# ScalarE's side work ahead of the products with v, maxima turned into rows where a phase opens, row tails copied by VectorE

## The chip, the cores and the metric

The kernel runs on one core of a Trainium2 chip. Its time is the device time of one execution in microseconds (us); lower is better. The engines of the core run side by side and meet at semaphores: TensorE (PE; PEld is its loading of weights), VectorE (DVE), ScalarE (ACT), GpSimd (POOL) and SyncE (SP), which here only issues DMAs.

## The reference

Attention over pooled queries feeds two gated or plain MLPs. The change touches the first part:

```python
q_pool = q.reshape(B, H, S // 2, 2, D).mean(axis=3)      # B=4, H=8, S=1152, D=64
scores = np.matmul(q_pool, k.transpose(0, 1, 3, 2)) / np.sqrt(D)
scores = scores - np.max(scores, axis=-1, keepdims=True)
attn = np.exp(scores)
attn = attn / (np.sum(attn, axis=-1, keepdims=True) + 1e-09)
out = np.matmul(attn, v)
# then: h = relu(x @ w_in); u, v = halves of h; v normed, mixed over time by w_spatial, u * that @ w_out
# then: u = x + (U V applied over time); out = u + relu(u @ w_ch1) @ w_ch2
```

The weights of the MLPs come in as 64-bit floats and are turned into pairs of 32-bit numbers on the chip.

## The kernel before

**Attention in pairs of heads.** 32 heads make 16 pairs (`j`, a *phase* of the program each). A pair has 576 pooled queries, in three thirds of 192 columns, so there are 48 units `u`; keys come in 9 chunks `c` of 128. The chunks of all units stand in one row, and four of them make a *group* `i` (108 groups). A group is two score tiles `s`: for each, 4 matmuls with k (L258) and 2 that take off the row of maxima `toprow` (L274, or L277 where two pairs meet), then an exponential on ScalarE (`expo`, L281) into `pt`. GpSimd adds up the `pt` tiles (`acc`, L288, L299, L302).

**Turns.** After every odd group come the products with v (`pv`, L309, 32 matmuls) of the two groups before it, and, where a unit ends, its sums (`sums`: L323 on TensorE, then the copy L327 on ScalarE). This text calls the stretch from one block of products to the next a *turn*: products, sums, a group, a group. VectorE inverts the sums in two halves (L331) and multiplies (`out`, L337) one turn later, which frees the bank `po`.

**Maxima.** The row of maxima is computed ahead, from rounded copies of q and k, in *pieces*: two matmuls of 512 columns (L171) and one maximum on VectorE (L193); a piece of the rest (L171 with 128 columns, in odd halves L201 too; L204, L213, L216, L217 on VectorE); and one over the query tail `qd` (L188, L189). `end` says how many pieces have to be done by a group, `some` places one. When a pair's maxima are there, `to_rows` turns them into a row: matmuls `tr` (L232, L239), a copy of 512 columns (L242) and two of the 64 tail columns (L249). Pieces, `tr` and score tiles share one ring of three PSUM slots, `ring`.

**Side work on ScalarE.** For the pair after next, `round_k` (L151) and `round_q` (L140, L145) copy k and the pooled q into the rounded form; `pool_q` (L134, GpSimd) makes that q. `also(i)` hands a tick to the preparation of the weights (`Weights.tick`): `phase` 0 is two ScalarE activations (L589, L590), 1, 2 and 4 are VectorE (L594, L598, L602), 3 is GpSimd (L600), 5 is a ScalarE copy (L674), 6 GpSimd (L679).

The order on every engine is the order in which this code is written (the schedule is manual), so an engine that waits holds up all that is written behind it. The MLP stages behind attention, from about 470 us on, are not touched.

Of the kernel before, what the change touches and what calls it, by code (L numbers as in the profile page):

```python
# [10 lines left out]
F32 = mybir.dt.float32  # L11
F32R = mybir.dt.float32r
ACTF = mybir.ActivationFunctionType
# [3 lines left out]
U32 = mybir.dt.uint32  # L17
# [20 lines left out]
def attention(tc, idf, q, k, v, xs, rounded, also):  # L38
# [13 lines left out]
    nc = tc.nc  # L52
    NP, D, _, _, T = q.shape
    S = k.shape[3]
    HP = NP // len(xs)
    KC = S // 128
# [13 lines left out]
    with ExitStack() as ctx, ExitStack() as sco:  # L70
# [14 lines left out]
        for e in range(2):  # L85
            p = slice(64 * e, 64 * e + 64)
# [23 lines left out]
        st = [dict() for _ in range(NP)]  # L110
# [19 lines left out]
        def pool_q(j, eng, c0=0, c1=T):  # L130
            s = st[j]
            if "q" not in s:
                s["q"] = ld.tile([128, T], F32, tag="q", name="q", bufs=3)
            eng.tensor_tensor(out=s["q"][:, c0:c1], in0=s["qraw"][:, 0, c0:c1], in1=s["qraw"][:, 1, c0:c1], op=ALU.add)  # L134

        def round_q(j, c0=0, c1=T):
            s = st[j]
            if "qr" not in s:
                s["qr"] = qrs[j % 2]
            nc.scalar.copy(s["qr"][:, c0:min(c1, 512)], s["q"][:, c0:min(c1, 512)])  # L140
            if c1 == T:
                s["qd"] = qds[j % 2]
                for e in range(2):
                    p = slice(D * e, D * e + D)
                    nc.scalar.copy(s["qd"][p, D * e:D * e + D], s["q"][p, 512:T])  # L145

        def round_k(j, c0=0, c1=S):
            s = st[j]
            if "kr" not in s:
                s["kr"] = krs[j % 2]  # L150
            nc.scalar.copy(s["kr"][:, c0:c1], s["k"][:, c0:c1])  # L151
# [6 lines left out]
        pieces = []  # L158
# [6 lines left out]
        upto = [sum(x[0] < u for x in pieces) for u in range(2 * NP + 1)]  # L165
# [55 lines left out]
        def to_rows(*us):  # L221

            j = us[0] // 2
            if us[0] % 2 == 0:
                st[j]["top"] = ld.tile([128, T], F32R, tag="toprow", name="toprow")
            t = st[j]["top"]
            rs = ring("tr")
            cs = [2 * (u % 2) + c for u in us for c in range(2)]
            for c in cs:
                for i in range(2):  # L230
                    p = slice(64 * i, 64 * i + 64)
                    nc.tensor.matmul(  # L232
                        rs[:, i, 64 * c:64 * c + 64], tops[j % 2][p, c].rearrange("p e d -> p (e d)"), idr[p],
                        start=True, stop=True,
                    )
            if us[-1] % 2:
                for i in range(2):
                    p = slice(64 * i, 64 * i + 64)
                    nc.tensor.matmul(  # L239
                        rs[:, i, 256:320], tops[j % 2][p, 4].rearrange("p e d -> p (e d)"), idr[p], start=True, stop=True  # L240
                    )
            nc.scalar.copy(  # L242
                t[:, 128 * cs[0]:128 * cs[-1] + 128].rearrange("p (c i x) -> p i c x", i=2, x=64),
                rs[:, :, 64 * cs[0]:64 * cs[-1] + 64].rearrange("p i (c x) -> p i c x", x=64),
            )
            if us[-1] % 2:
                for i in range(2):
                    p = slice(64 * i, 64 * i + 64)
                    nc.scalar.copy(t[p, 512:T], rs[p, i, 256:320])  # L249

        def scores(pair):

# [120 lines left out]
        groups = [chunks[i:i + G] for i in range(0, len(chunks), G)]  # L373

        at = [3 * KC * j // G for j in range(NP)]
        before = []

        smalls = {}
# [9 lines left out]
        j = 0  # L388
        for i, group in enumerate(groups):
            if j + 1 < NP and at[j + 1] == i:  # L390
                j += 1
            r = i - at[j]
            if r == 0:
                if j + 2 < NP:
                    load_k(j + 2)
                    load_q(j + 2)
                if j + 1 < NP:
                    load_v(j + 1)

            end = min(upto[2] + -(-upto[2] * (4 * (i | 1) + 8) // (3 * KC)), upto[2 * NP])  # L400
            if i < len(FIRST):
                end = min(end, FIRST[i])

            def some(beside=False, lag=0):
                if done[0] < end - lag:
                    piece(beside=beside)

            new = []
            if i == 2:
                new = [1]  # L410
            elif r == 0 and j:
                new = [2 * j, 2 * j + 1]
            for u in new:
                while done[0] < upto[u + 1]:
                    piece()
            if new:
                to_rows(*new)
            elif i % 2 == 0:
                some(True)
            for x in smalls.pop((i, 0), ()):  # L420
                x()
            ts = []
            for x in range(0, G, W):
                pair = group[x:x + W]
                ts.append((pair, scores(pair)))
                if i == 0 and x + W == G:
                    some()
                if i or x + W == G:
                    for y in ts:
                        less(*y)  # L430
                        expo(*y)
                    ts = []
            if i < len(FIRST):
                some(bool(i % 2))
            elif i % 2 == 0:
                some(lag=1)
            else:
                some(done[0] + 1 >= end)
                some(True)

            for _ in range(2 if i < 4 else 0):
                if done[0] < end:
                    piece(ps_s.tile([128, 2, 512], F32, tag="s", name="r1"))
            for x in smalls.pop((i, 1), ()):
                x()
            if i + 1 == len(groups):
                break
            if i == 0:
                round_q(1)
                round_k(1)  # L450
            if i % 2:
                for x in before:
                    pv(*x)
                before = []
                for u in sums_at.pop(i, ()):
                    sums(u)
            before = before + group
            also(i)
            if r == 2 and j + 2 < NP:
                pool_q(j + 2, nc.gpsimd)  # L460

            if r == 3 and j + 2 < NP:
                round_k(j + 2)
            if r == 4 and j + 2 < NP:
                round_q(j + 2)
        sco.close()
        for x in before:
            pv(*x)
# [30 lines left out]
class Weights:  # L499
# [5 lines left out]
    def __init__(self, nc, stages, most=1 << 30, keep=None):  # L505

        self.nc, self.stages, self.most, self.keep = nc, stages, most, keep
        self.units, self.free = [], []
        self.time = self.begun = self.loaded = self.staged = 0

        self.apart = 2

        self.late = 0

    def load(self, units=(), raws=()):

# [53 lines left out]
    def work(self, u, phase):  # L574

        nc = self.nc
        if phase == 5:  # L580
            u["hi"](u["st"])
        elif phase == 6:
            u["lo"](u["st"])
        elif not u["f32"]:
            lo, hi = u["raw"][:, :, 0], u["raw"][:, :, 1]
            if phase == 0:
                u["st"] = self.stages[self.staged % len(self.stages)][0:u["p"], 0:u["n"]]
                self.staged += 1
                nc.scalar.activation(u["st"], hi.bitcast(F32), ACTF.Abs, scale=2.0**-48)  # L589
                nc.scalar.activation(lo, lo.bitcast(U32), ACTF.Copy, scale=2.0**-29)  # L590
            st = u["st"]
            o = st.bitcast(I32)
            if phase == 1:
                nc.vector.tensor_scalar(  # L594
                    out=st, in0=st, scalar1=LEAST, scalar2=MOST, op0=ALU.max, op1=ALU.min, accum_out=LOWEST[0][0:st.shape[0]]
                )
            elif phase == 2:
                nc.vector.tensor_scalar(out=o, in0=o, scalar1=3, scalar2=None, op0=ALU.logical_shift_left)  # L598
            elif phase == 3:
                nc.gpsimd.tensor_tensor(out=o, in0=o, in1=lo, op=ALU.add)  # L600
            elif phase == 4:
                nc.vector.scalar_tensor_tensor(  # L602
                    out=o, in0=hi, scalar=-0x80000000, in1=o, op0=ALU.bitwise_and, op1=ALU.bitwise_or
                )
# [79 lines left out]
def gated_mlp(tc, idf, w_in, w_sp, b_sp, w_out, wU, wV, xs, us, last, soon, then, spill):  # L684
# [104 lines left out]
    w = Weights(nc, stages, keep=LAST)  # L789
    w.apart = 4  # L790
    w.late = 1

    yield yh.rearrange("p a t d -> p (a t d)")
    nc.gpsimd.memset(f(wst[64:128, 1, NT - 1]), 0.0)
    i = 0
    while not isinstance(i, str):
        if i == WEIGHTS:
            w.load(units, raws)
        if i >= WEIGHTS + 2:
            w.tick()  # L800
        if i == X_AT:
            load_x(0)
        i = yield
    w.end()

    e2 = room(right, "e2", side="right")
# [595 lines left out]
```

## Time and profile before

| | |
|---|---|
| median of 3 runs | 1123.17 us (1122.11 to 1123.65) |
| the profiled execution | 1123.47 us, of which the span 1121.5 us |
| PE busy over the span | 1103.0 us (98%) |
| PEld, DVE, ACT, POOL busy | 956.2, 578.1, 446.8, 541.1 us |
| chain that ended last | PE 50% of the span, no other engine over 3% |

Matmuls overlap in TensorE's pipeline, so a busy row has stretched matmuls in it too; a wait of TensorE shows first in its loading of weights, which runs ahead of the matmuls. A timeline row is: start, length, engine, line, operation, tiles and shapes, count, and in brackets the engine's idle time ahead of it with what ended it.

### The profile page before, as it was taken

The page shows a single profiled execution, that of the slowest core. Times are in us where ns is not written, and L with a number is a line of the kernel's source. Part 1 is how long each engine was busy: PE and PEld are TensorE (multiplying, and loading weights), DVE is VectorE, ACT ScalarE, POOL GpSimd, SP SyncE. Part 2 cuts the span into 40 slices and gives each one's busy share as a digit, 9 for nine tenths or more (in the row PEclk, how much of TensorE's full clock was granted, in tenths as well). Part 3 has the DMA queues.
Part 4 walks back from the last instruction along what each step waited for, and adds up shares of the span by engine and source line. Part 5 has one row for each costly group of instructions (what it writes and reads, how often), then busy time and mean ns, then how long its engine had stood idle before and what let it go on. Part 6 is the DMA issues. An engine that isn't in the chain of part 4 may idle for free.

```text
span 1121.5 us, 20408 instructions
## 1 busy us (share of the span) xinstructions
PE 1103.0 (98%) x8406; PEld 956.2 (85%) x8406; DVE 578.1 (52%) x933; ACT 446.8 (40%) x824; POOL 541.1 (48%) x421
## 2 busy tenths in 40 slices
PE   8999999999999999999999999999999999999998
PEld 6878878888778888798988989899998999999897
DVE  6767877766777785353465653469412121121211
ACT  4455565555665554452343443356311111111110
POOL 4678899898799796534364545357300000000000
PEclk9999999999999999999999999999999999999999
DMA  6334333325334311022233406345102010010000
GB/s 169 90 89 114 103 100 103 82 70 135 98 98 135 82 36 37 12 69 91 84 114 111 139 29 193 99 137 164 48 1 85 1 57 1 1 57 1 29 1 29
DMA packets 44847, 86.65 MB, mean 77 GB/s; under 512 B 6353, under 2 KB 21329, under 8 KB 44754
## 3 DMA queue, kind: packets, MB, share of 16 engines
q1 hardware_dynamic: 44754, 85.35, 25.8%
q8 instruction: 66, 1.08, 0.4%
q14 instruction: 27, 0.22, 0.1%
HBM read 66.98 MB, written 17.83 MB: 76 GB/s over the span
## 4 chain that ended last, share of the span: by engine, by line
PE 50%; DVE 3%; ACT 1%; DMA 1%; POOL 1%; issue 1%; SPq 0%; ACTq 0%; POOLq 0%; DVEq 0%
PE ph L1245 18%; PE py L1259 18%; PE py L1025 4%; PE pu L973 3%; PE pg L991 3%; PE pv L838 2%; DMA cw<-st 1%; PE pU L1008 1%; PE pt L1237 1%; DVE st L664 1%; POOL st L662 1%; PE pV L1050 1%; DVE bs L933 1%; POOL gt L491 0%; DVE xt L491 0%
## 5 line engine op out<-in xcount | busy, mean ns | idle before, releaser
L1245 PE MATMUL ph<-ut,w 128*128 128x384 f32 x1152 | 216.9, 336 | 0.0
L1259 PE MATMUL py<-w,h 128*128 128x512 f32 x864 | 216.7, 395 | 0.0
L1245 PEld LDWEIGHTS ph<-ut,w 128*128 128x128 f32 x1152 | 203.9, 188 | 8.4
L1249 DVE SCALAR_TENSOR_TENSOR h<-ph,h 128x384 fp32r<-128x384 f32 x96 | 53.5, 557 | 284.6 <-ACT h L1248 284.6
L281 ACT ACTIVATE pt<-s 128x768 f32<-128x768 f32 x216 | 172.0, 811 | 60.4 <-PE s L274 56.7
L193 DVE TENSOR_REDUCE m<-r 128x2 f32<-128x1024 f32 x128 | 154.9, 1222 | 76.0 <-PE r L171 75.8
L299 POOL TENSOR_TENSOR acc<-pt,acc 128x768 f32<-128x768 f32 x94 | 173.7, 1848 | 37.4 <-ACT pt L281 31.9
L258 PE MATMUL s<-q,k 64*128 64x192 f32 x1728 | 184.8, 332 | 1.5 <-DVE m L193 0.7
L1259 PEld LDWEIGHTS py<-w,h 128*128 128x128 f32 x864 | 159.9, 188 | 29.8
L1248 ACT ACTIVATE h<-ph 128x384 fp32r<-128x384 f32 x96 | 47.2, 492 | 301.7 <-PE ph L1245 300.1
L258 PEld LDWEIGHTS s<-q,k 64*128 64x128 f32 x1728 | 142.8, 187 | 18.0 <-ACT pt L281 9.3
L309 PE MATMUL po<-pt,v 128*64 128x192 f32 x1728 | 154.2, 330 | 1.0 <-DVE x L337 0.9
L309 PEld LDWEIGHTS po<-pt,v 128*64 128x64 f32 x1728 | 118.8, 137 | 31.1 <-issue 13.7
L299 POOL TENSOR_TENSOR acc<-pt 128x768 f32<-128x768 f32 x48 | 88.1, 1836 | 33.0 <-ACT pt L281 32.8
L274 PE MATMUL s<-toprow,yh 64*128 64x384 f32 x416 | 99.1, 470 | 1.0 <-ACT toprow L242 1.0
L331 DVE RECIPROCAL sum<-sum 128x96 f32<-128x96 f32 x96 | 70.8, 742 | 32.8 <-ACT sum L327 32.8
L171 PE MATMUL r<-yh 64*128 64x512 f32 (+1 forms) x384 | 68.2, 384 | 5.1 <-ACT pt L281 5.0
L327 ACT ACTIVATE sum<-po 128x192 f32<-128x192 f32 x48 | 15.9, 331 | 140.8 <-PE po L323 102.5
L991 PE MATMUL pg<-wst,vn 128*128 128x288 f32 x448 | 60.6, 295 | 0.6 <-DVE ut L997 0.6
L991 PEld LDWEIGHTS pg<-wst,vn 128*128 128x128 f32 x448 | 59.7, 188 | 1.0 <-DVE ut L997 0.9
L171 PEld LDWEIGHTS r<-yh 64*128 64x128 f32 x384 | 35.2, 185 | 24.7 <-ACT pt L281 11.7
L973 PEld LDWEIGHTS pu<-xt,wi 128*128 128x128 f32 x384 | 53.3, 188 | 2.1
(153 smaller groups left out, 1345.1 us busy)
## 6 DMA issues: line engine op xcount, KB each, us to landing
raw<-in_moe_w_ch_dram SPq DMA_DIRECT2D x28, 512.0 KB, 3.8
v<-in_v_dram SPq DMA_DIRECT2D x16, 576.0 KB, 4.1
qraw<-in_q_dram SPq DMA_DIRECT2D x30, 288.0 KB, 5.6
k<-in_k_dram SPq DMA_DIRECT2D x30, 288.0 KB, 4.5
x<-x SPq DMA_DIRECT2D x48, 96.0 KB, 2.2
xn<-x SPq DMA_DIRECT2D x4, 1152.0 KB, 5.8
out_dram<-un SPq DMA_DIRECT2D x18, 256.0 KB, 2.1
raw<-in_moe_w_in_dram SPq DMA_DIRECT2D x8, 512.0 KB, 5.9
```

What stands on the lines that cost most here:

```text
L171: nc.tensor.matmul(o, s["qr"][p, q0:q0 + 128], s["kr"][p, k0:k0 + n], start=True, stop=True)
L193: nc.vector.tensor_reduce(out=m[:, c, :, k0 // PW], in_=r, axis=AX.X, op=ALU.max, negate=True)
L258: nc.tensor.matmul(t[:, e, N * x:N * x + N], s["k"][p, 128 * c:128 * c + 128], s["q"][p, q0:q0 + N], start=x == 0, stop=False,)
L274: nc.tensor.matmul(t[:, e, 0:2 * N], first[p], m, start=False, stop=True)
L281: nc.scalar.activation(x, t[:, :, 0:W * N], ACTF.Exp, scale=SC)
L299: nc.gpsimd.tensor_tensor(out=a, in0=x, in1=jb["t"] if c < 4 else a, op=ALU.add)
L309: nc.tensor.matmul(jb["o"][D * e:D * e + D, 0:N], st[u // 3]["v"][:, e, c], jb["p", c][:, e], start=c == 0, stop=c == KC - 1,)
L331: nc.vector.reciprocal(out=t, in_=t)
L973: nc.tensor.matmul(p[:, 0:HT], wi[0][:, a, k, 128 * m:128 * m + 128], xt[:, c, k, HT * h:HT * h + HT], start=i == 0, stop=i == 3 * KD - 1,)
L991: nc.tensor.matmul(p[:, 0:HT], vn[:, a, s, 128 * m:128 * m + 128], wst[:, c, s, sl], start=s == 0 and i == 0, stop=s == NT - 1 and i == 1,)
L1245: nc.tensor.matmul(p[:, 0:BT], w1s[m][:, a, k], ut[i][:, c, k], start=j == 0, stop=j == 3 * KD - 1)
L1259: nc.tensor.matmul(py[i][c], h[:, a, 128 * c:128 * c + 128], w2s[m][:, e], start=m == 0 and a + e == 0, stop=m == KM - 1 and a == 1,)
```

## The change

In `attention`, at the end of an odd group, the weights' tick, `round_k` and `round_q` (now both in the same odd group of a phase, r = 3 or 4) are written ahead of the products with v; before, they stood behind the products and the sums. In `Weights`, phases 0 and 5 of a tick don't issue their ScalarE instructions at once: `on_act` holds them, and `also(None)` issues what is held, which happens only in odd groups, ahead of the tick and again ahead of the products. `to_rows` is called only in an even group, right behind the products of the turn before (`turns`), with no piece between; a phase that opens with an odd group gets its row one group earlier. The pieces are due a group earlier (12 for 8 in `end`), and none is placed before its pair is rounded. The row's tail columns are copied by VectorE.

```diff
-                    nc.scalar.copy(t[p, 512:T], rs[p, i, 256:320])
+                    nc.vector.tensor_copy(out=t[p, 512:T], in_=rs[p, i, 256:320])
...
+        turns = {i - i % 2: j for j, i in enumerate(at) if j}
...
-            end = min(upto[2] + -(-upto[2] * (4 * (i | 1) + 8) // (3 * KC)), upto[2 * NP])
+            end = min(upto[2] + -(-upto[2] * (4 * (i | 1) + 12) // (3 * KC)), upto[2 * NP])
...
-                if done[0] < end - lag:
+                if done[0] < end - lag and "qr" in st[pieces[done[0]][0] // 2]:
                     piece(beside=beside)
...
-            elif r == 0 and j:
-                new = [2 * j, 2 * j + 1]
+            elif i in turns:
+                new = [2 * turns[i], 2 * turns[i] + 1]
...
             if i % 2:
+                also(None)
+            also(i)
+            if r == 2 and j + 2 < NP:
+                pool_q(j + 2, nc.gpsimd)
+            if r == 3 + at[j] % 2 and j + 2 < NP:
+                round_k(j + 2)
+                round_q(j + 2)
+            if i % 2:
+                also(None)
                 for x in before:
                     pv(*x)
                 before = []
                 for u in sums_at.pop(i, ()):
                     sums(u)
             before = before + group
-            also(i)
-            if r == 2 and j + 2 < NP:
-                pool_q(j + 2, nc.gpsimd)
-
-            if r == 3 and j + 2 < NP:
-                round_k(j + 2)
-            if r == 4 and j + 2 < NP:
-                round_q(j + 2)
...
+    def act(self):
+        for x in self.held:
+            x()
+        self.held = []
+
+    def on_act(self, x):
+        if self.held is None:
+            x()
+        else:
+            self.held.append(x)
...
         if phase == 5:
-            u["hi"](u["st"])
+            self.on_act(lambda: u["hi"](u["st"]))
...
+        if i is None:
+            w.act()
+        elif i >= WEIGHTS + 2:
             w.tick()
```

(Phase 0 goes through `on_act` in the same way; behind attention the held list is emptied and switched off.)

On ScalarE, around the opening of the pair with groups 13 to 19; before, two groups of exponentials (L281, two tiles each) with side work between them:

```order
L151 CAST yh<-k 128x1152
L281 ACTIVATE pt<-s 128x768 x2
L589 ACTIVATE st_114<-raw_110 128x512
L590 ACTIVATE raw_110<-raw_110 128x512
L140 CAST yh<-q 128x512
L145 CAST yh<-q 64x64 x2
L281 ACTIVATE pt<-s 128x768 x4
L242 CAST toprow<-tr 128x2x4x64
L249 CAST toprow<-tr 64x64 x2
```

The same place after; the exponentials of a turn stand together, side work stands behind them and ahead of the copy of the sums, L242 stands ahead of a turn's exponentials, and L249 is gone from this engine:

```order
L281 ACTIVATE pt<-s 128x768 x4
L151 CAST yh<-k 128x1152
L140 CAST yh<-q 128x512
L145 CAST yh<-q 64x64 x2
L327 ACTIVATE sum<-po 128x192
L281 ACTIVATE pt<-s 128x768 x4
L606 ACTIVATE st_114<-raw_110 128x512
L607 ACTIVATE raw_110<-raw_110 128x512
L242 CAST toprow<-tr 128x2x4x64
L281 ACTIVATE pt<-s 128x768 x4
```

On TensorE in the turn with groups 12 and 13, before, from the last products on (the `tr` of the phase stands between its two groups, behind a piece; numbers tell the buffers apart):

```order
L309 MATMUL po_843<-pt_791,v_277 64x192 x4
L171 MATMUL r_861<-yh_95 128x512 x2
L258 MATMUL s_866<-q_212,k_170 128x192 x4
L274 MATMUL s_866<-toprow_576,yh_95 128x384 x2
L258 MATMUL s_878<-q_212,k_170 128x192 x4
L274 MATMUL s_878<-toprow_576,yh_95 128x384 x2
L171 MATMUL r_888<-yh_95 128x512 x2
L232 MATMUL tr_902<-yh_95 128x64 x8
L239 MATMUL tr_902<-yh_95 128x64 x2
L258 MATMUL s_916<-q_212,k_170 128x192 x4
```

After, the `tr` stands right behind the products, and the piece between products and scores is gone from there:

```order
L309 MATMUL po_844<-pt_794,v_277 64x192 x4
L232 MATMUL tr_862<-yh_95 128x64 x8
L239 MATMUL tr_862<-yh_95 128x64 x2
L258 MATMUL s_876<-q_212,k_170 128x192 x4
L274 MATMUL s_876<-toprow_576,yh_95 128x384 x2
L258 MATMUL s_888<-q_212,k_170 128x192 x4
L274 MATMUL s_888<-toprow_576,yh_95 128x384 x2
L171 MATMUL r_898<-yh_95 128x512 x2
```

Of the 15 rows of maxima that are made after the first, 8 move like this; the other 7 stood there already. GpSimd and SP run the same instructions in the same order as before. TensorE runs the same matmuls.

On VectorE, after, at a later opening: the two tail copies stand behind the weights' work (L613, L621) and ahead of the first half of the next inversion.

```order
L337 TENSOR_TENSOR x<-po,sum 128x192
L193 TENSOR_REDUCE m<-r 128x2
L613 TENSOR_SCALAR pair,lowest<-pair 128x512
L621 SCALAR_TENSOR_TENSOR st_115<-raw_111,st_115 128x512
L249 CAST toprow<-tr 64x64 x2
L331 RECIPROCAL sum<-sum 128x96
```

Before, the same stretch has no L249; the rest of it is as it was.

## Rows read from the trace of the kernel before

**Rows 1.** Windows: start and end, length, busy and count by engine, clock, DMA.

```profile
40.00:470.00 430.00, 423.08 (x4651) 350.22 (x4650) 303.54 (x448) 242.90 (x408) 357.16 (x234) 1.00 0.33 90
```

**Rows 2.** Waits before 470 us, PEld: who waited for whom, total us, times, longest.

```profile
PEld r L171 <- ACT pt L281: 11.7, 21, 1.8
PEld r L171 <- issue: 11.1, 41, 0.3
PEld s L258 <- ACT pt L281: 9.3, 35, 0.4
PEld po L309 <- DVE x L337: 2.6, 5, 0.9
PEld s L274 <- ACT toprow L242: 2.1, 4, 1.1
```

**Rows 3.** The same view from 40 to 470 us.

```profile
PEld r L171 <- ACT pt L281: 8.3, 15, 1.8
```

**Rows 4.** Timeline of the second half of one turn, 60 to 67 us.

```profile
60.67 0.33 ACT L327 ACTIVATE sum<-po 128x192 f32<-128x192 f32 x1 [3.48 <-PE po L323]
61.02 1.15 ACT L151 CAST yh<-k 128x1152 fp32r<-128x1152 f32 x1
...
63.48 0.66 ACT L589 ACTIVATE st<-raw 128x512 f32<-128x512 f32 x1
...
64.05 0.68 ACT L590 ACTIVATE raw<-raw 128x512 int32<-128x512 uint32 x1
...
64.62 0.60 ACT L140 CAST yh<-q 128x512 fp32r<-128x512 f32 x1
...
65.13 0.49 ACT L145 CAST yh<-q 64x64 fp32r<-64x64 f32 x2
...
65.64 1.51 ACT L281 ACTIVATE pt<-s 128x768 f32<-128x768 f32 x2
...
66.51 0.44 PE L171 MATMUL r<-yh 64*128 64x128 f32 x4 [1.42 <-ACT pt L281]
```

**Rows 5.** Timeline, a row of maxima between two groups, 132 to 134 us.

```profile
132.43 0.57 ACT L242 CAST toprow<-tr 128x512 fp32r<-128x512 f32 x1
...
132.90 0.43 ACT L249 CAST toprow<-tr 64x64 fp32r<-64x64 f32 x2
133.05 0.44 PE L274 MATMUL s<-toprow,yh 64*128 64x384 f32 x2 [0.81 <-ACT toprow L242]
```

**Rows 6.** Windows, each one turn.

```profile
83.16:90.93 7.77, 7.77 (x87) 6.50 (x87) 7.42 (x9) 4.18 (x7) 7.01 (x5) 1.00 0.54 156
57.10:66.99 9.89, 8.41 (x94) 6.94 (x93) 7.07 (x8) 6.35 (x12) 8.02 (x6) 1.00 0.31 105
66.99:74.95 7.96, 7.88 (x90) 6.58 (x89) 5.46 (x11) 3.56 (x8) 3.64 (x3) 1.00 0.01 2
143.12:150.25 7.13, 7.13 (x79) 5.92 (x79) 3.69 (x4) 3.25 (x6) 7.05 (x6) 1.00 0.06 20
225.42:233.20 7.78, 7.78 (x88) 6.50 (x87) 5.46 (x7) 3.27 (x5) 7.62 (x6) 1.00 0.41 126
184.01:192.52 8.51, 8.51 (x98) 7.04 (x96) 6.26 (x12) 5.86 (x11) 7.73 (x6) 1.00 0.45 119
```

**Rows 7.** ScalarE's longest waits before 470 us.

```profile
ACT sum L327 <- PE po L323: 102.5, 35, 4.2
```

**Rows 8.** Timeline, GpSimd's pooled q and what follows on ScalarE, 284 to 289 us.

```profile
284.65 1.42 POOL L134 TENSOR_TENSOR q<-qraw 128x576 f32<-128x576 f32 x1
...
286.94 0.33 ACT L327 ACTIVATE sum<-po 128x192 f32<-128x192 f32 x1 [2.77 <-issue]
...
288.21 1.65 ACT L281 ACTIVATE pt<-s 128x768 f32<-128x768 f32 x2
```

**Rows 9.** Timeline of VectorE behind the last piece of a pair.

```profile
67.10 0.69 DVE L204 TENSOR_REDUCE m<-r 128x4 f32<-128x512 f32 x1 [0.75 <-PE r L201]
67.71 0.27 DVE L213 TENSOR_REDUCE md<-r 64x1 f32<-64x128 f32 x1
...
68.67 0.17 DVE L217 TENSOR_REDUCE yh<-m 128x4 fp32r<-128x12 f32 x1
```

**Rows 10.** Timeline, one VectorE instruction of the weights at two times.

```profile
108.27 0.36 DVE L598 TENSOR_SCALAR pair<-pair 128x512 int32<-128x512 int32 x1
...
158.47 2.00 DVE L598 TENSOR_SCALAR st<-st 128x512 int32<-128x512 int32 x1
```

More of the change, by code (lines that the diff above doesn't have):

```diff
@@ L517, in __init__ @@
         self.late = 0
+        self.held = None
+    def act(self):
[7 more added lines that the diff above has]
+            self.held.append(x)
     def load(self, units=(), raws=()):
@@ L588, in work, with begin @@
                 self.staged += 1
-                nc.scalar.activation(u["st"], hi.bitcast(F32), ACTF.Abs, scale=2.0**-48)
-                nc.scalar.activation(lo, lo.bitcast(U32), ACTF.Copy, scale=2.0**-29)
+                def begin():
+                    nc.scalar.activation(u["st"], hi.bitcast(F32), ACTF.Abs, scale=2.0**-48)
+                    nc.scalar.activation(lo, lo.bitcast(U32), ACTF.Copy, scale=2.0**-29)
+                self.on_act(begin)
             st = u["st"]
@@ L791, in gated_mlp @@
     w.late = 1
+    w.held = []
     yield yh.rearrange("p a t d -> p (a t d)")
@@ L798, in gated_mlp @@
             w.load(units, raws)
-        if i >= WEIGHTS + 2:
+        if i is None:
+            w.act()
+        elif i >= WEIGHTS + 2:
             w.tick()
@@ L803, in gated_mlp @@
         i = yield
+    w.act()
+    w.held = None
     w.end()
```

## The prediction

> **What bounds the kernel now.** I read four views: the windows of the stages, to see who is full; TensorE's waits, as its weight loads show them; single turns, to see what a wait adds to one; and the timeline around the longest waits. From 40 to 470 us, where the change lies, TensorE is busy for 423.08 of 430 us; the others stand at 357 (GpSimd), 304 (VectorE) and 243 (ScalarE) [rows 1]. So TensorE sets the pace, its matmuls stay the same, and all there is to win is the time in which it stands. The weight loads name the causes [rows 2]: pieces (L171) that wait for an exponential, 11.7 us in 21; score matmuls for an exponential, 9.3 in 35; L274 for the row of maxima, 2.1 in 4; the products for VectorE's multiplication, 2.6 in 5. The reader has to take a floor off: 41 pieces stand for 11.1 us although nothing holds them ("issue"), 0.27 us each [rows 2], which no order of ScalarE removes. The 35 waits of the score matmuls are 0.27 us each as well, so I count no gain there.
>
> The timeline shows why the others are long [rows 4]. ScalarE stands for 3.48 us until the sums are done, then copies them and takes k (1.15 us). Between its two groups of exponentials come L589, L590, L140 and L145, from 63.48 to 65.62 us. The second group starts at 65.64, its slots of the ring come free late, and the last piece of the turn waits: TensorE idles 1.42 us. Side work is done when TensorE needs exponentials, and ScalarE stands while TensorE does the products. The waits of the sums' copies come to 102.5 us over 35 of them [rows 7]: that is the room into which the change puts the side work.
>
> **The change part by part.** *Side work ahead of the products.* Each turn's exponentials now run without side work between them. The pieces' waits go down to their floor. From 40 us on: 8.3 - 15 x 0.27 = 4.2 us [rows 2, 3]. Before 40 us: 11.7 - 8.3 = 3.4 us in 6, above the floor 1.8; about half of them lie in the opening groups, whose order hardly changes, so I take 0.9, between 0 and 1.8.
>
> Does the room suffice? The heaviest turn has L589, L590, L151, L140 and L145: 0.66 + 0.68 + 1.15 + 0.60 + 0.49 = 3.58 us [rows 4]. ScalarE's idle time ahead of a sums' copy is 2.9 us in the mean (102.5 / 35) [rows 7] and 3.48 in the turn shown, so the heaviest block can hold the copy back by 0.1 to 0.7 us. But the copy (0.33 us) isn't what TensorE needs: behind the sums come a piece and a score tile before the next exponential is due, and between the copy and that exponential lie 1.27 us (286.94 to 288.21) [rows 8], 0.94 of them free. So the cost is nought while that cover stands; without it, 0 to 0.7 us in the few heaviest turns, some 4 of them. I take 0.3 us in all, and up to 2.8.
>
> The held activations reach VectorE later: the first weight instruction of VectorE waits for the first activation of the block, 0.66 us behind the exponentials, and behind it on VectorE stand the other weight step and the next turn's maxima, which can't begin before the products end. Nobody on TensorE waits for it. The copy of phase 5 has GpSimd's subtraction behind it, at the end of a queue that is still adding exponentials. Nought, and nothing below nought.
>
> *The pooled q.* `round_q` now follows GpSimd's sum by one group in some phases and two in others; it was two. In the turn shown the sum ends at 286.07; ScalarE would be there at about 285.2, wait 0.9, and do L140 and L145 (1.09 us) until 287.2. The copy of the sums then ends by 287.5, and the next exponentials were due at 288.21: 0.7 us left [rows 4, 8]. Nought here; the fourth case below has its price.
>
> *Rows of maxima.* Where `tr` stands between the groups, ScalarE's L242 comes behind side work: L274 waits 0.81 us for it [rows 5], 2.1 us in all four [rows 2]. In the new place L242 stands behind a copy of the sums only. Gain 2.1 us. The position itself: a turn with `tr` between its groups takes 7.96, one with as many pieces and without `tr` 7.13, both without sums: 0.83 us. With `tr` at its head a turn takes 8.51, without 7.78, both with sums: 0.73 us [rows 6]. So 8 moves gain 8 x 0.10 = 0.8 us; at most a whole floor of a ring wait each, 8 x 0.27 = 2.2. Against that: the maxima must be ready when the products end. Behind the last piece VectorE needs from 67.10 to 68.84 us, 1.74, and up to one more maximum of a piece ahead of it [rows 9]. The products alone take 2.8 us, with sums 3.6. Only one of the 8 moved rows has its last piece directly ahead of products without sums; I put 0.2 us on it, between 0 and 0.5.
>
> *Tails on VectorE.* ScalarE gets rid of 0.43 us per row [rows 5], within the gains above. VectorE has no such copy in the trace: 0.17 us (L217, little data) and 0.69 (L204, 512 columns from PSUM) bound one [rows 9]; I take 0.27, that of L213, which reads 64 partitions of PSUM as the copy does. 30 of them make 8 us on an engine with 126 us free [rows 1]. They wait for `tr` at the head of a turn, and what stands behind them (the inversions) waits for sums that end just ahead of `tr`. Nought, if VectorE isn't late; rival two prices that.
>
> *Pieces a group earlier.* Their number is the same; nought, with 0.2 us either way where two follow one another.
>
> **Sum.** 4.2 + 0.9 + 2.1 + 0.8 = 8.0 us gained; 0.3 + 0.2 lost; 7.5 net. The profiled execution took 1123.47 us (a span of 1121.5 and 2.0 around it), 0.3 above the median: 1123.47 - 7.5 = 1116.0, and for the median 1115.7.
>
> A check by turns: the turn of the timeline took 9.89 us; one with the same pieces but the last took 7.77 [rows 6], and that piece took 0.48 (66.51 to 66.99). So 1.64 us went astray, where the weight load shows 1.79 - 0.27 = 1.52, the 1.8 being the longest wait [rows 2]. A stall is some 0.12 us dearer than the loads tell; with 19 stalls after 40 us the upper end of the gain is 8.0 + 0.9 + 1.4 + 2.3 = 12.6, less what is lost, about 12.
>
> The matmul row alone would say less: it is idle for 430 - 423.08 = 6.9 us [rows 1], and that is the most that any order could bring there. The Trainium skill (Perfetto Trace Analysis, Identifying the Most-Contended Engine) says that busy matmuls are no good measure of headroom since they are pipelined, and that the share of weight loads is to be taken. By that share, 350.22 of 430, there would be some 80 us of room; the turn of 7.77 us, without any stall, has its weight loads at 6.50, so most of that room is not there, and the waits of the loads are the better view.
>
> **The rivals.** *One, the forecast:* stalls by ScalarE go, the rest stays. 1112 to 1118.5.
>
> *Two, VectorE takes the place.* The pieces and the products wait for VectorE too (2.6 us in 5 for the multiplication [rows 2]). One of its weight steps took 0.36 us and the same step 2.00 at another time [rows 10]; the multiplication stands behind it. With exponentials earlier and VectorE's own queue as long as before plus the tails, half of the pieces' gain (2.5) could be lost to it and these waits double (2.6): 7.5 - 5.1 = 2.4, so 1120.8. For it: VectorE was busy for 7.42 of the 7.77 us of a turn [rows 6]; against it: TensorE was not held up in that turn. The Trainium skill (SBUF — State Buffer, Who interferes with whom) says that VectorE's `tensor_scalar` in a two-port mode and GpSimd lock one another out for a whole instruction; the two lengths agree with it, and GpSimd's additions now fall at other times.
>
> *Three, the stalls are the floor.* The waits named after exponentials are then ring waits that any order has. 1122.5 to 1123.5. Against it: turns of 7.77 and 7.78 us with three pieces and no stall [rows 6].
>
> *Four, slower: ScalarE blocked by GpSimd's pooled q.* ScalarE is in order, and behind `round_q` now stand the sums' copy and the next exponentials. 13 phases have it. There are 0.7 us left in the turn shown; if the pooled q ended L us later, each phase would lose L - 0.7. It eats the gain from L = 0.7 + 7.5 / 13 = 1.3 us on, and at 1.6 us the loss is 13 x 0.9 = 11.7: 1123.2 + 4.2 = 1127.4. For it: GpSimd is the second fullest engine [rows 1]. Against it: its order is unchanged, and the exponentials it waits for come earlier.
>
> **How the numbers follow.** Forecast 0.62, two 0.20, three 0.11, four 0.07. The predicted time is 1115.7 us. The range goes from 1111.8 (the upper gain) to 1121.5, rival two with 0.7 us of slack; it leaves out three and four and the best end. A measurement of this kernel can tell 0.2%, 2.2 us, from no change: faster is below 1120.9. The forecast and most of two (0.18) are there: 0.80; within 0.2% the rest of two and three: 0.13; slower 0.07.
>
> **What would show it.** In the new trace the weight loads of pieces wait for exponentials at 0.3 us each and no longer, L274 waits for no row, ScalarE's idle time ahead of the sums' copies falls by some 60 us, and the turn with three pieces and a rest piece takes about 8.2 us for 9.89. Wrong would be: waits of ScalarE for L134, waits of `tr` for L217, or longer waits of the products for L337. The stages behind attention should be shifted, not changed.

## The result and the profile after

| | before | after |
|---|---|---|
| median | 1123.17 us (1122.11 to 1123.65) | 1113.32 us (1112.91 to 1114.39, 5 runs) |
| the profiled execution | 1123.47 us, span 1121.5 us | 1114.39 us, span 1112.6 us |

The ratio is 0.9916, with a 95% interval of 0.9902 to 0.9929: 9.85 us less, faster by more than the 0.2% that can be told. The forecast was 1115.7 us in a range of 1111.8 to 1121.5.

Where the time went shows in the products with v, the first and the last block of attention (line L309 by itself: count, duration in ns, first and last start), of before and then of after:

```profile
L309 PE MATMUL po<-pt,v x1728: 326/326/580, 22.1 to 474.5; 128*64 128x192 f32 x192
```

```profile
L309 PE MATMUL po<-pt,v x1728: 326/326/377, 23.4 to 465.0; 128*64 128x192 f32 x192
```

From the first product to the last it took 452.4 us and now 441.6, 10.8 less. The opening began 1.3 us later in this execution (last section), and the stages behind attention gave back 0.6 of the 9.5 that were left: the span is 8.9 shorter.

The page of after, busy time by engine, and the window that answers to [rows 1]:

```profile
PE 1098.7 (99%) x8406; PEld 955.9 (86%) x8406; DVE 582.7 (52%) x965; ACT 449.6 (40%) x792; POOL 541.0 (49%) x421
```

```profile
40.00:463.00 423.00, 421.72 (x4669) 351.95 (x4666) 310.02 (x485) 246.33 (x379) 357.67 (x235) 1.00 0.34 91
```

TensorE stands for 1.28 us of 423, where it stood for 6.9 of 430. The two windows don't end at the same place of the program; from the first product to the last (windows, before and after) it stood for 7.9 us and now for 1.8:

```profile
22.10:474.50 452.40, 444.52 (x4840) 366.11 (x4840) 318.67 (x466) 252.38 (x424) 368.86 (x242) 1.00 0.32 86
```

```profile
23.40:465.00 441.60, 439.77 (x4838) 365.67 (x4838) 322.31 (x498) 254.66 (x392) 369.26 (x242) 1.00 0.32 88
```

The weight loads, for [rows 2] (waits up to 463 us: who for whom, total us, times, longest):

```profile
PEld po L309 <- issue: 12.7, 44, 0.4
PEld s L258 <- ACT pt L281: 8.9, 33, 0.3
PEld r L171 <- ACT pt L281: 8.2, 25, 1.1
PEld r L171 <- issue: 8.2, 31, 0.3
PEld tr L232 <- issue: 4.8, 17, 0.3
...
PEld po L309 <- DVE x L337: 1.2, 2, 1.0
...
PEld s L274 <- ACT toprow L242: 0.2, 1, 0.2
```

The pieces' waits for exponentials were 11.7 us in 21, so 0.56 each; now they are 0.33 each, near the floor of 0.27. L274 has all but stopped waiting. The waits for the multiplication (L337) were halved, which I had not counted on.

The turn that stood longest before, 9.89 us [rows 6], is now this one (window), and ScalarE in it (timeline) answers to [rows 4]:

```profile
57.60:65.83 8.23, 8.23 (x93) 6.89 (x92) 6.05 (x8) 5.83 (x10) 6.61 (x5) 1.00 0.31 108
```

```profile
58.02 1.15 ACT L151 CAST yh<-k 128x1152 fp32r<-128x1152 f32 x1
60.09 0.62 ACT L140 CAST yh<-q 128x512 fp32r<-128x512 f32 x1 [0.92 <-POOL q L134]
60.62 0.49 ACT L145 CAST yh<-q 64x64 fp32r<-64x64 f32 x2
61.17 0.33 ACT L327 ACTIVATE sum<-po 128x192 f32<-128x192 f32 x1
62.42 1.64 ACT L281 ACTIVATE pt<-s 128x768 f32<-128x768 f32 x2 [0.93 <-PE s L274]
64.49 1.64 ACT L281 ACTIVATE pt<-s 128x768 f32<-128x768 f32 x2 [0.42 <-PE s L274]
```

The side work stands between 58.02 and 61.1 us, beside the products; between the two groups of exponentials there is none, and ScalarE waits for TensorE instead of the other way round. The wait for GpSimd's pooled q that the fourth rival rests on is there (0.92 us), and 0.93 us are still left ahead of the next exponential.

One long stall is left in attention, and it is VectorE's (timeline, 302 to 305 us):

```profile
302.08 3.79 POOL L299 TENSOR_TENSOR acc<-pt,acc 128x768 f32<-128x768 f32 x2
...
302.38 1.82 DVE L617 TENSOR_SCALAR st<-st 128x512 int32<-128x512 int32 x1
...
304.12 0.35 DVE L337 TENSOR_TENSOR x<-po,sum 128x192 f32<-128x192 f32 x1
...
304.52 1.20 PE L309 MATMUL po<-pt,v 128*64 128x192 f32 x12 [0.69 <-DVE x L337]
```

A weight step (L617) takes 1.82 us beside GpSimd's additions; the multiplication stands behind it, and the products behind that.

### The profile page after: what moved, and what is told of

Read it like the earlier page. It is cut to its first block, busy times and chain, and to the rows that moved or that the text cites. A ratio compares the mean times of both kernels' runs of the same rounds, so it can differ in the third digit from the quotient of the medians.

```text
span 1112.6 us, 20415 instructions
## 1 busy us (share of the span) xinstructions
PE 1098.7 (99%) x8406; PEld 955.9 (86%) x8406; DVE 582.7 (52%) x965; ACT 449.6 (40%) x792; POOL 541.0 (49%) x421
## 4 chain that ended last, share of the span: by engine, by line
PE 50%; DVE 3%; ACT 1%; DMA 1%; issue 1%; POOL 1%; SPq 0%; ACTq 0%; POOLq 0%; DVEq 0%
PE ph L1269 18%; PE py L1283 18%; PE py L1049 4%; PE pu L997 3%; PE pg L1015 3%; PE pv L862 2%; DMA cw<-st 1%; PE pU L1032 1%; PE pt L1261 1%; DVE st L683 1%; POOL st L681 1%; PE pV L1074 1%; DVE bs L957 1%; DVE xt L493 0%; POOL gt L493 0%
## 5 line engine op out<-in xcount | busy, mean ns | idle before, releaser
L281 ACT ACTIVATE pt<-s 128x768 f32<-128x768 f32 x216 | 175.2, 812 | 79.1 <-PE s L274 75.1
L309 PE MATMUL po<-pt,v 128*64 128x192 f32 x1728 | 153.2, 329 | 0.7 <-DVE x L337 0.7
L309 PEld LDWEIGHTS po<-pt,v 128*64 128x64 f32 x1728 | 118.9, 137 | 29.2 <-issue 13.1
L274 PE MATMUL s<-toprow,yh 64*128 64x384 f32 x416 | 98.6, 468 | 0.0
L997 PE MATMUL pu<-xt,wi 128*128 128x288 f32 x384 | 54.4, 294 | 0.0
```

Source lines behind the costliest of these rows:

```text
L274: nc.tensor.matmul(t[:, e, 0:2 * N], first[p], m, start=False, stop=True)
L281: nc.scalar.activation(x, t[:, :, 0:W * N], ACTF.Exp, scale=SC)
L309: nc.tensor.matmul(jb["o"][D * e:D * e + D, 0:N], st[u // 3]["v"][:, e, c], jb["p", c][:, e], start=c == 0, stop=c == KC - 1,)
L997: nc.tensor.matmul(p[:, 0:HT], wi[0][:, a, k, 128 * m:128 * m + 128], xt[:, c, k, HT * h:HT * h + HT], start=i == 0, stop=i == 3 * KD - 1,)
```

## The experiments

Each kernel was timed beside the kernel before on the same chip; the ratio is to that, with its 95% interval. There were three such sets, in which before took 1123.29 us (side_only, rows_only, pieces_8, tails_scalar), 1123.00 (behind, no_hold, q_late, x_early) and 1123.11 (the others). "After" or "before" says which kernel the edit starts from. A in the quoted expectations is the forecast's cause; the other letters are told there by what they expect.

| kernel | side work ahead | pieces earlier (12) | rows at a turn's head | tails on VectorE | median us | ratio |
|---|---|---|---|---|---|---|
| side_only | yes | | | | 1116.61 | 0.9939 [0.9925, 0.9952] |
| due_only | | yes | | | 1136.08 | 1.0117 [1.0100, 1.0133] |
| rows_place_only | | | yes | | 1125.95 | 1.0026 [1.0017, 1.0035] |
| rows_only | | yes | yes | | 1133.50 | 1.0089 [1.0075, 1.0103] |
| pieces_8 | yes | | yes | yes | 1120.25 | 0.9969 [0.9958, 0.9981] |
| side_due | yes | yes | | | 1114.55 | 0.9924 [0.9909, 0.9939] |
| tails_scalar | yes | yes | yes | | 1114.28 | 0.9917 [0.9904, 0.9931] |
| after_again (after) | yes | yes | yes | yes | 1113.77 | 0.9915 [0.9900, 0.9930] |

**side_only**: from after, with everything undone but the side work.

```diff
-            end = min(upto[2] + -(-upto[2] * (4 * (i | 1) + 12) // (3 * KC)), upto[2 * NP])
+            end = min(upto[2] + -(-upto[2] * (4 * (i | 1) + 8) // (3 * KC)), upto[2 * NP])
...
-            elif i in turns:
-                new = [2 * turns[i], 2 * turns[i] + 1]
+            elif r == 0 and j:
+                new = [2 * j, 2 * j + 1]
```

(and L249 back on ScalarE; the condition that a piece is not placed before its rounding stays)

> The changed kernel with rows of maxima, due numbers of the pieces and tail copies as before: only ScalarE's side work moves ahead of the products. Theory A (stalls by side work between the exponentials make most of the gain): the waits of pieces for exponentials fall to their floor of 0.27 us, L274 waits for no row although tr still stands between two groups, and 6.5 to 8 us of the 9.85 are there: 1115 to 1117. Rival B (the place of the rows and pieces makes it): at most 3 us, 1120 or more.

Measured: 6.7 us less than before, of the 6.5 to 8 expected. Its weight loads:

```profile
PEld r L171 <- ACT pt L281: 7.1, 21, 1.1
...
PEld po L309 <- DVE x L337: 2.8, 5, 0.9
```

The 21 waits are the same in number as before and 4.6 us shorter. L274's 2.1 us are gone here too (0.2 in one), although the rows stand between the groups as before: they were a cost of the side work ahead of L242, not of the rows' place.

**rows_only**: from before, with the rest of the change but the tails (rows at a turn's head, 12 for 8, no piece ahead of its rounding).

```diff
+        turns = {i - i % 2: j for j, i in enumerate(at) if j}
...
-            end = min(upto[2] + -(-upto[2] * (4 * (i | 1) + 8) // (3 * KC)), upto[2 * NP])
+            end = min(upto[2] + -(-upto[2] * (4 * (i | 1) + 12) // (3 * KC)), upto[2 * NP])
...
-                if done[0] < end - lag:
+                if done[0] < end - lag and "qr" in st[pieces[done[0]][0] // 2]:
...
-            elif r == 0 and j:
-                new = [2 * j, 2 * j + 1]
+            elif i in turns:
+                new = [2 * turns[i], 2 * turns[i] + 1]
```

> The kernel before with the rows of maxima at the head of an even group's turn and the pieces due a group earlier; side work and tail copies stay on ScalarE as before. Theory A: the waits of pieces for exponentials stay at 8 us or more after 40 us, the waits for the row go, 1 to 3 us of gain: 1120 to 1122. Rival B: 7 us or more, 1116 or less.

Measured: 10 us more than before, which neither theory had. Its weight loads:

```profile
PEld r L171 <- ACT pt L281: 21.3, 30, 1.8
...
PEld r L171 <- ACT yh L140: 8.1, 9, 1.3
```

A new wait, for the rounding of q (L140), and nearly twice the old one. The next two kernels took this one apart.

**due_only** and **rows_place_only**: from before, each with one half of that edit (12 for 8 with the condition on "qr"; or `turns` alone).

> The kernel before with the pieces due a group earlier (12 for 8, none before its pair is rounded); rows, side work and tails as before. Theory H (the 10 us that the rows and pieces alone cost come from pieces that meet a rounding which is not done: ScalarE has L140 in order behind its exponentials): waits of pieces for L140 of 4 to 8 us and 1127 to 1134. Rival I (the rows at the head of a turn cost it): no such waits, 1121 to 1125.

> The kernel before with the rows of maxima at the head of an even group's turn alone; pieces due as before, side work and tails as before. Theory H: two openings have the last piece ahead of tr (2 us each, as in pieces_8), against that the moved rows gain 2 to 4: 1121 to 1125. Rival I: 1128 or more.

Measured: the earlier pieces alone cost 13 us, more than in company with the rows and above the 1127 to 1134 expected; the rows' place alone costs 2.8, just above its range, and gained nothing. The weight loads of due_only hold 10.7 us in 11 waits for the rounding, where 4 to 8 were expected:

```profile
PEld r L171 <- ACT pt L281: 18.5, 26, 1.8
...
PEld r L171 <- ACT yh L140: 10.7, 11, 1.3
```

Above the floor of 0.27 us each these two rows come to 11.5 + 7.7 = 19.2 us; before had 6.0, all of it in the first. The 13.2 more account for the 13 us of the time. TensorE and ScalarE in due_only (timeline), at one of eight such places:

```profile
95.57 0.33 ACT L327 ACTIVATE sum<-po 128x192 f32<-128x192 f32 x1 [2.14 <-PE po L323]
95.80 0.61 ACT L140 CAST yh<-q 128x512 fp32r<-128x512 f32 x1
```

```profile
94.65 0.82 PE L323 MATMUL po<-acc,ones 128*64 128x192 f32 x8
96.46 0.50 PE L171 MATMUL r<-yh 64*128 64x512 f32 x2 [1.00 <-ACT yh L140]
```

The first piece of the new pair stands right behind the sums, and the rounding that it reads stands behind the copy of the same sums. That is the order of before, and there the piece came a group later.

**pieces_8**: from after, with 8 for 12 in `end`.

> The changed kernel with the pieces due as before (8 for 12 in end). At two of the openings the last piece of the pair then stands between the products and tr, so that tr waits for VectorE's chain behind that piece, 1.74 us in the trace of before. Theory A: those two turns get 1.3 to 2 us longer, nothing else: 1115.5 to 1117.5. Rival D (the due numbers matter everywhere, since VectorE needs the lead): more openings have waits of tr for L217, 1119 or more.

Measured: 6.9 us above after, and 6.0 above tails_scalar, which was timed beside it. That is the time of D, while the waits for L217 stand at the two openings of A. Timeline of one of the two long turns, behind its products:

```profile
149.07 0.44 PE L171 MATMUL r<-yh 64*128 64x128 f32 x4
...
149.85 0.68 DVE L204 TENSOR_REDUCE m<-r 128x4 f32<-128x512 f32 x1
...
151.41 0.17 DVE L217 TENSOR_REDUCE yh<-m 128x4 fp32r<-128x12 f32 x1
...
151.63 0.41 PE L232 MATMUL tr<-yh 64*128 64x64 f32 x4 [1.82 <-DVE yh L217]
```

The last piece stands directly ahead of `tr`, and VectorE's chain of 1.7 us (149.85 to 151.58) lies open. The two turns account for 3.5 us (2 waits of TensorE for L217 from 40 us on); waits for L337 in the loads went from 1.2 us in 2 to 2.6 in 4; the rest is not followed. So the rows at the head need the earlier pieces, and rows_place_only shows the same wait for L217 (3.3 us in 2).

**side_due**: from after, with the rows between the groups again and L249 on ScalarE.

> Side work ahead of the products and the pieces due a group earlier; rows between the groups as before, tails on ScalarE. Theory H: with the rounding done in time the due numbers cost nothing, no wait of a piece for L140 over 0.3 us: 1115.5 to 1118, as with the side work alone. Rival I': the due numbers cost by themselves, 1120 or more.

Measured: 1114.55, 2 us better than side_only and below the range (the runs of the two don't overlap, their intervals do a little). With the side work ahead, the earlier pieces cost nothing and seem to bring a little. The waits of pieces for L140 are 1.2 us in 3, the longest 0.6 where 0.3 was expected. Against tails_scalar, which differs from it by the place of the rows alone, it is 0.3 us, which these runs can't tell from nothing.

**tails_scalar**: from after, L249 back on ScalarE.

```diff
-                    nc.vector.tensor_copy(out=t[p, 512:T], in_=rs[p, i, 256:320])
+                    nc.scalar.copy(t[p, 512:T], rs[p, i, 256:320])
```

> The changed kernel with the two tail copies of a row on ScalarE again. Theory A: 15 x 0.43 us more on ScalarE ahead of a turn's exponentials, where some 0.9 us are free: within 1 us of the changed kernel, 1113 to 1114.5. Rival C (at the head of a turn ScalarE has no room): each of the 15 rows holds the exponentials up by 0.2 to 0.4 us, 3 to 6 us: 1116.5 to 1119.

Measured: 1114.28, beside 1113.32 and 1113.77 for after, with intervals that overlap almost wholly. The tails are worth nothing that can be measured. This kernel makes another pair, too: rows_only, timed in the same set, differs from it by the place of the side work alone and took 1133.50, so with rows and pieces in their new places that is worth 19.2 us.

**behind**: from after, the products and sums written ahead of the side work again.

```diff
             if i % 2:
                 also(None)
+                for x in before:
+                    pv(*x)
+                before = []
+                for u in sums_at.pop(i, ()):
+                    sums(u)
             also(i)
...
                 also(None)
-                for x in before:
-                    pv(*x)
-                before = []
-                for u in sums_at.pop(i, ()):
-                    sums(u)
```

> The changed kernel with ScalarE's side work (weights' tick, k, q, in the same odd groups) behind the products and sums again; rows, pieces and tails as in the changed kernel. Theory A (side work has to fill the time of the products): it now stands between the sums' copy and the next exponentials, 1.6 us per turn in the mean and 3.6 in the heaviest where 0.9 are free, so the gain is gone: 1122 to 1135, with score tiles and pieces waiting for exponentials. Rival B (the place of rows and pieces makes the gain): 1113 to 1116.

Measured: 1155.08, 1.0289 [1.0275, 1.0304], and so 42 us above after: the order of these few lines is worth far more in the new arrangement than the whole change, since the earlier pieces rely on it. The expected 1122 to 1135 was too low. This is not the old order of the side work, which was spread over odd and even groups; that one, with the rows and pieces of after, is rows_only. TensorE's waits:

```profile
PE r L171 <- ACT yh L140: 13.8, 7, 3.1
PE s L258 <- ACT pt L281: 5.3, 6, 1.1
PE r L171 <- DVE toprow L249: 4.2, 3, 2.3
```

**no_hold**: from after without the held list, so the weights' activations are issued in any group again.

```diff
-    w.held = []
...
-            w.act()
+            pass
...
-    w.act()
-    w.held = None
```

> The changed kernel without the held list: the weights' ScalarE instructions are issued at their tick, so those of even groups stand between a turn's two groups of exponentials again; k, q and the odd ticks stay ahead of the products. Theory A: some 16 turns have L606 and L607 (1.3 us) in the way, of which about 0.5 are hidden, each 0.2 to 0.8 us: 3 to 10 us more, 1116.5 to 1123. Rival E (only the longer blocks with k and q hurt): within 1 us of the changed kernel.

Measured: 1117.70, 0.9953 [0.9941, 0.9966], 4 us above after, inside the range of A. The pieces' waits for exponentials, 8.2 us in 25 in after, are back in part (loads):

```profile
PEld r L171 <- ACT pt L281: 11.2, 24, 1.1
```

**q_late**: from after, GpSimd's pooled q written right ahead of the rounding, so behind one or two more groups of additions. It prices the fourth rival.

```diff
-            if r == 2 and j + 2 < NP:
-                pool_q(j + 2, nc.gpsimd)
             if r == 3 + at[j] % 2 and j + 2 < NP:
+                pool_q(j + 2, nc.gpsimd)
                 round_k(j + 2)
```

> The changed kernel with GpSimd's pooled q issued right ahead of the rounding that reads it, one or two groups later than in the change. Theory A with the price of the fourth case: ScalarE waits for L134 some 2 us longer in each of 13 phases than it does in the change (0.2 to 0.9 us there in three), of which 0.7 are hidden: 13 x 1.3 = 17 us more, 1125 to 1133. Rival F (the sums' copy and exponentials have far more slack): ScalarE waits as long, but the time stays within 2 us of the changed kernel.

Measured: 1173.03, 1.0438 [1.0422, 1.0454], 60 us above after; 1125 to 1133 was expected. GpSimd, ScalarE and TensorE at the longest wait (timelines, 92 to 101 us):

```profile
97.75 1.40 POOL L134 TENSOR_TENSOR q<-qraw 128x576 f32<-128x576 f32 x1
```

```profile
99.18 0.62 ACT L140 CAST yh<-q 128x512 fp32r<-128x512 f32 x1 [7.05 <-POOL q L134]
```

```profile
92.92 0.82 PE L323 MATMUL po<-acc,ones 128*64 128x192 f32 x8
99.85 0.80 PE L171 MATMUL r<-yh 64*128 64x512 f32 x2 [6.10 <-ACT yh L140]
```

ScalarE's waits for L134 come to 62.9 us in 15. From 40 to 515 us TensorE stands for 41.4 us, and it works at a lower clock behind the longest wait (last section).

**x_early**: from after, the multiplication of a unit (`out`, L337) a little earlier: at the end of the even group, right behind the inversion and ahead of the weight step that held it up, and no longer at the head of the odd group behind that step.

```diff
-                    smalls.setdefault((at_sum + 2, 0), []).append(lambda u=u: out(u))
+                    smalls.setdefault((at_sum + 1, 1), []).append(lambda u=u: out(u))
```

> The changed kernel with VectorE's multiplication (L337) right behind the second half of its inversion, at the end of the even group, ahead of the weights' step L617 that took 1.82 us ahead of the one stall left in attention. Theory G: the products' waits for L337 go, 0.7 to 1.2 us less: 1112.1 to 1112.8. Rival: another instruction of VectorE is late in its place, 1113 to 1114.

Measured: 1112.16 us (1111.98 to 1112.33), 0.9904 [0.9890, 0.9917]. The stall shown above is gone (timeline):

```profile
301.27 0.36 DVE L337 TENSOR_TENSOR x<-po,sum 128x192 f32<-128x192 f32 x1
301.54 1.40 DVE L617 TENSOR_SCALAR st<-st 128x512 int32<-128x512 int32 x1
...
301.72 2.82 PE L309 MATMUL po<-pt,v 128*64 128x192 f32 x32
```

Its median is the lowest of all and lies outside the runs of after and, barely, of after_again (1112.19 to 1114.42); the intervals overlap, so 1.2 us is what the medians say, not what is certain.

**after_again**: after once more, for the late opening.

> The changed kernel once more, on the chip of these runs, so that its parts can be set against it: 1112.9 to 1114.4 by every theory; a profile without a late start of the first pooled q (10.44 us in its first profile, 9.99 before) has a span about 1 us shorter than the first.

Measured: 1113.77 us. In its profile the opening is in time, and the span is 1112.6 us all the same; beside the stall of 0.7 us for L337 that both have, it has two late stalls that the first profile doesn't have (TensorE's waits from 40 us on):

```profile
PE r L171 <- DVE m L193: 1.0, 2, 0.8
```

So one profile of this kernel differs from the next by about 1 us in where it stands, and I draw nothing from less.

## Why the prediction was right, point by point

**The cause holds.** TensorE set the pace and stood for ScalarE's side work. side_only undoes everything else and keeps 6.7 of the 9.85 us; undoing the side work alone, with rows and pieces left as in after, loses 19.2 (tails_scalar to rows_only). The turn of 9.89 us was to take about 8.2 and takes 8.23.

**Terms that held.** The pieces' waits above the floor were to give 5.1 us in the loads (4.2 + 0.9): 11.7 - 21 x 0.27 = 6.0 before and 8.2 - 25 x 0.27 = 1.5 now, so 4.6. L274 was to give 2.1 and gave 1.9. The room ahead of the sums' copies sufficed.

**Terms that were mis-sized.** The waits for L337 were left unchanged and fell from 2.6 to 1.2 us. The position of `tr` was put at 0.8 us; side_due against tails_scalar leaves 0.3, within the spread. In the loads of before, `tr` waited 3.8 us in 14:

```profile
PEld tr L232 <- issue: 2.4, 9, 0.3
PEld tr L232 <- ACT pt L281: 1.4, 5, 0.3
```

After, it is 4.8 us in 17, all at the floor, while pieces wait as often as before (60 and 59 times from the first product to the last, by all their rows); so in the loads the new place of `tr` gains nothing. The pair of turns on which I built 0.10 us per move (8.51 and 7.78) was not a clean one, since the former also has two pieces in a row.

**Waits that the sum left out.** The forecast's 7.5 us came from two rows of the loads and the place of `tr`, and 9.85 were measured. From the first product to the last, all waits of the weight loads (every row of that view added up) come to 62.7 us in 193 before and 51.4 in 176 after: 11.3 less, for 10.8 us of time. Pieces, by all their rows, gave 5.1 of it and L274 with L277 2.3, about as forecast. The products gave 2.0, the score tiles 1.2 and the pieces of the query tail 1.2, which the prediction had at nothing, and `tr` lost 0.8 where it was to gain as much; no run takes these apart. The same sum follows the time in the parts: 6.9 us less for 7.2 in side_only, 9.6 more for 9.3 in rows_only, 12.0 more for 12.0 in due_only. So at a granted clock of 1.00 stalls are not dearer than the loads tell, as the check by turns had it (0.12 us each, from one turn); more kinds of waits shrank than the sum had. The floor of 0.27 us, which no order of ScalarE was to remove, is paid by 17 waits fewer. The matmul row said less, as predicted: its idle time fell by 6.05 us, and the other 4.75 are matmuls that are no longer stretched (444.5 us busy, now 439.8).

**The range.** Its lower end, 1111.8, is 11.4 us below the median of before, while the check by turns had put the upper gain at about 12; the measurement is 1.5 us above that end.

**The term that holds in company only.** The pieces a group earlier were put at nought because their number is the same. But the first of a pair reads the rounded q, and they are nought, or some 2 us to the good (side_only to side_due), only where the rounding of q and k stands ahead of the products. In the old order they cost 13 us, and without them the rows' new place costs 6 to 7 (pieces_8). The sum added edits that aren't independent: alone they read -6.7, +13.0 and +2.8, together -9.85. The sum of the prediction came out near because its terms were read in the company of the whole change; they would have misled whoever made only a part of it.

**Credit to the wrong edit.** The 2.1 us of L274 were put down to the rows' new place. side_only has them too.

**ScalarE's idle time** ahead of the sums' copies was to fall by some 60 us. Before, it was 102.5 us [rows 7] and a second row that isn't among them; after, the two read:

```profile
ACT sum L327 <- PE po L323: 75.0, 31, 3.9
ACT sum L327 <- issue: 17.4, 8, 2.7
```

Before, that second row was:

```profile
ACT sum L327 <- issue: 30.9, 12, 3.4
```

That is 133.4 us before and 92.4 after, 41 less (27.5 less by the row of [rows 7] alone). The direction is right, and the size was a guess of how much side work had stood elsewhere.

**The rivals.** Two (VectorE takes the place) didn't come: its waits shrank, and the 30 tails cost nothing. But the stall that is left is its, at the instruction that the rival named, and x_early removes it. Three (the stalls are the floor) is refuted. Four (the pooled q) did not decide here: ScalarE waited 0.92, 0.52 and 0.21 us in three phases, which the prediction had named as a sign of being wrong, and no piece of TensorE waited longer than 0.3 us for L140 or L145 behind the opening. Its price was wrong by far, though. I gave each phase 0.7 us of slack, up to the next exponential. In the phases where a piece stands right behind the sums, it reads the rounded q at once, and there is next to none: in q_late a wait of 7.05 us on ScalarE became one of 6.10 on TensorE, and the lower clock behind it (below) came on top.

## What to carry to other kernels

Put side work of an in-order engine where the engine that sets the pace does long work that doesn't need it, and look for that place in the waits of the side engine, not in its busy share. When a change moves producers and consumers together, price every part with the others absent as well: here the earlier consumers alone cost 13 us, the earlier producers alone gained 6.7. The slack of a moved instruction ends at the first reader of anything behind it, so follow all its readers, not the one that was late before. And add up every wait in front of the weight loads, not only those for which a cause is at hand.

## What the hardware showed that was not expected

**A stall costs more than its length.** Behind the stand of 6.10 us in q_late the granted clock is at half, the 1.2 GHz level, and the same matmuls take longer until it is back at 2.4 GHz (window, then timeline):

```profile
99.00:103.00 4.00, 3.15 (x20) 3.06 (x21) 1.88 (x2) 1.99 (x5) 0.14 (x1) 0.50 0.00 0
```

```profile
103.07 0.78 PE L274 MATMUL s<-toprow,yh 64*128 64x384 f32 x2
...
105.05 0.47 PE L274 MATMUL s<-toprow,yh 64*128 64x384 f32 x2
```

From 40 to 515 us of that kernel the clock's mean is 0.95 and TensorE stands for 41.4 us, of a loss of 60. In behind, the clock is 0.63 from 98 to 100 us, behind a stand of 2.56. The short stalls in attention of before and after left it at 1.00 in the mean. The late opening in the profile of after goes with the same: the first pooled q came at 10.44 us for 9.99 (GpSimd waited for its DMA), the first piece on it waited 1.42 us for 0.93, and from 12.0 to 14.2 us the clock was 0.61, where before had 1.00.

**One VectorE instruction, many lengths.** In attention, L617 (the L598 of [rows 10]) took from 0.36 us (four times) to 1.82 on a 128x512 tile of after. In the stall shown, it began at 302.38, 0.3 us into the first of GpSimd's two additions (some 1.9 us each), and ended at 304.20, about 0.2 us behind the end of that addition. The seven others of more than 0.36 us each end 0.27 or 0.28 us behind the end of a GpSimd instruction, such as the one of 1.59 us that ends at 173.57 where an addition ends at 173.29. The Trainium skill (SBUF — State Buffer, Who interferes with whom) says that VectorE in a two-port mode and GpSimd hold the shared ports for a whole instruction, and that the other is blocked meanwhile; the trace agrees with it here. Which mode L617 ran in no row shows.

**A copy that waits for another engine's copy.** L249 on VectorE reads another part of `tr` than L242 on ScalarE, and yet it begins only behind the end of that copy, at 45.41 us here (timeline of after):

```profile
45.44 0.46 DVE L249 CAST toprow<-tr 64x64 fp32r<-64x64 f32 x2 [2.08 <-ACT toprow L242]
```

Of the 2.08 us of idle time 0.59 is L242 itself. Both write the tile `toprow` and both read `tr`; which of the two orders them no run shows. In after, what stood behind it on VectorE had time, so it cost nothing, but moving a copy to another engine did not take it out of the first one's queue: where L242 came late, pieces waited for L249, 4.2 us in behind (shown there) and 7.1 in q_late.
